# Attention into a feed-forward layer on one core: PSUM tiles handed out by the kernel, single-bank tiles for the block-form layer, one load cut into three, and a new order for every engine

## The chip, the cores and the metric

The kernel runs on one core of one Trainium2 chip. A core has a matrix engine (TensorE, PE in the profile), a vector engine (VectorE, DVE), an activation engine (ScalarE, ACT), GpSimd (POOL), which in this kernel issues the loads, and SyncE (SP), which issues transposing DMAs, copies and stores. Matmuls write to PSUM, a small memory of 128 partitions with eight banks of 512 fp32 values each; ACT and DVE read PSUM and write to SBUF. The metric is device time in microseconds (us). The kernel before takes 366.14 us, the median of three runs (365.94 to 366.96).

## The reference

```python
scores = (1/sqrt(64)) * q @ k.T             # q, k, v: 8 batches x 12 heads x 448 x 64, fp32
attn   = maximum(scores, 0)**2 / 448        # relu squared, no softmax
x      = (attn @ v).transpose(0, 2, 1, 3).reshape(3584, 768)
h      = x @ w_in                           # w_in: 768 x 2048
out    = gelu_exact(h) @ w_out              # w_out: 2048 x 768
```

Nothing is routed: every token goes through the same two layers. The kernel computes in bf16 with fp32 sums.

## The kernel before, in words

**Attention.** A batch has 12 heads in three groups of four (g = 0, 1, 2); below, (b, g) is group g of batch b. The loads of k, q and v (`add_k` L553, `add_q` L464, `add_v` L571) are cast to bf16 by the DMAs that POOL issues. q and k have to be turned so that the 64 head elements lie on the partitions. For batches 0 and 1 PE turns them and ACT or DVE copies the result out of PSUM (L520, L518). For batches 2 to 7 SP issues transposing DMAs (`turn`, L667), and the two halves of the turned q are swapped into a second copy (`swapped`): either by two DMAs of SP (L688, L689) or by two copies on DVE (L518). One attention step, "QK", is four matmuls of 448 columns (L744) into one two-bank PSUM tile; then relu with its scale on ACT (L756) or DVE (L758), then the square as a product on DVE (L765). Seven steps make a group of heads, whose 28 matmuls with v ("AV", L805) fill another two-bank tile; two copies (ACT L520 or DVE L518) bring it to x. Batch 0 is worked on in two halves of its queries, h0 and h1; its first q halves are loaded group by group, its second q halves by one load of 336 KB, `add_q(0, 0, G, HC, NC)`. In its own cost for a load (`add_q`) the kernel adds 390e3 bytes, one us at the rate that it assumes, to a load of this form.

**First layer.** Batches 0 to 3 are computed plainly: "F1", six matmuls of 448 columns for each of 16 blocks of 128 outputs (L857), then gelu on ACT (L867). Batches 4 to 7 use a block form of two by two blocks with seven products instead of eight (`add_blocks`, `add_block`, L1009). A block pair (b, m4) has two halves y = 0 and 1, and each half has three sums a, b, c that take in the products one after another; after each product DVE or ACT reads the sum (L1046, L520) before the next product is added to it. The gelu is L1055. The inputs are sums of blocks of x (`xs`) and of w_in (`ws`, L927), made on DVE.

**Second layer.** 14 row groups of 256 tokens. The first is done plainly (L1295), the others in the same seven-product form (`add_group`): eight matmuls for each product (L1191), copies and additions on ACT and DVE (L520, L1225), and stores issued by SP (L1145). Single-bank tiles come from the pool `f_pp` (two).

**PSUM.** The pool `w_pp` (L430) has three tiles of two banks, for QK, AV and the block form. `f_pp` (L431) has two tiles of one bank. In the block form, the two halves y of a sum share a tile of `w_pp`, one bank each; the tile comes free when both halves have been read (`joint`).

**The order.** The kernel is written as a list of operations (`sch.add`), and a string `ORDER` names every one of them in sequence: a letter for the engine (P, A, D, G for POOL, S) and the operation's number. `Scheduler.place` replays it, so each engine works through its operations in the string's order; within it an engine waits at the first one whose inputs are not ready. The string was made from the scheduler's own costs. With it PE alternates QK steps, AV and matmuls of the layers of earlier batches, so that relu and squares of one step run beside the layers' matmuls. POOL's loads wait in its queue, too: at most eight DMAs of POOL are under way at a time.

The lines of the code that set this:

```python
    w_pp = pool("w_pp", 3, PS)
    f_pp = pool("f_pp", 2, PS)
...
    add_q(0, 0, G, HC, NC)
    add_win(0)
    add_win(1)
```

Of the kernel before, what the change touches and what calls it, by code (L numbers as in the profile page):

```python
# [19 lines left out]
NA = 14  # L20
HP = H // 2
# [65 lines left out]
G0 G1 G3 G4 G1470 G7 A10 D13 A16 G121 P11 G2 P17 D12 D18 G117 P14 P42 D15 P39 G6 A43 P21 A40 P33  # L87
D22 P36 D44 P19 A37 P23 D20 G118 A34 D24 P25 G122 P54 D41 A26 G5 A55 P66 P57 Z1056 D67 A58 P63
P27 P29 A64 P69 D30 P48 D59 P31 A70 D28 D38 P78 A49 P51 D35 P133 G8 A52 D50 P45 D68 A79 P81 D53
A134 D46 P75 D47 G9 D65 A32 P131 A82 D56 P111 D132 A76 P108 D112 P129 G125 A109 D71 P102 P84 D103  # L90
G126 A85 P72 D80 P60 A73 D130 G120 A74 P93 D77 A61 P135 D104 A62 P96 D110 P105 A97 P141 D106 G147
A94 G124 D98 P165 A142 P90 P168 D107 A166 P143 D113 D86 A91 D83 P114 G119 A169 D92 P87 D115 A144
D95 A116 P171 D88 P137 A172 D89 P99 D138 A136 P159 P156 G128 D100 P145 D160 A157 D101 P162 A146
D173 P174 P186 G148 D175 P251 A187 D167 P243 A252 D170 A163 D158 P183 D188 A244 P189 P195 G150
P259 D184 A196 G154 A190 D176 P253 G151 D164 A260 G153 D161 P139 D191 P180 A140 P198 P177 D181
A199 D185 A254 P219 P216 G123 A178 P245 A220 G127 D179 S229 D182 P247 A246 A217 S228 P210 A248
P204 D218 P207 P263 A208 D205 P261 D211 A264 D197 S232 P192 A262 P213 D200 P222 A214 P255 D209
S231 A223 D193 P257 A256 D215 S235 P267 D206 A258 D194 S234 D221 P249 A268 D224 D212 P201 A250
P225 D230 G270 A202 A203 G238 P276 P279 A226 G149 D277 P265 A227 G239 A280 D233 P294 A266 P288
P291 A295 G152 P356 A289 P348 G272 G269 G271 P303 P285 A357 A292 A349 P350 A304 A286 P354 A351  # L100
D287 P312 P300 A355 P318 S399 P362 D281 D313 D296 P364 A363 D319 P370 D278 A301 A365 P358 A371
P315 P306 A359 P282 P352 D307 P360 A353 G241 P376 A361 P368 A377 A283 P366 A369 D284 D302 D236
# [82 lines left out]
class Scheduler:  # L185
# [170 lines left out]
    def place(self, fixed):  # L356
# [21 lines left out]
        while rest or any(fixed.values()):  # L378
# [16 lines left out]
            else:  # L395
                rest.remove(op)


@with_exitstack
def kernel(  # L400
    ctx: ExitStack,
# [388 lines left out]
    def add_av(blk, bias):  # L790
# [42 lines left out]
        if b in (B - 3, B - 1):  # L833
            old = [o for (bb, *_), o in AV.items() if bb == b - 1]
# [725 lines left out]
```

## Time and profile before

| what | value |
|---|---|
| runs | 366.14 us median of 3 (365.94 to 366.96) |
| span of the profiled execution | 365.2 us; its own time is some 0.9 us more, if it is taken for a median run (366.14 - 365.2) |
| PE busy | 356.2 us, 98% of the span, 3598 matmuls |
| DVE busy | 297.5 us, 81% |
| ACT busy | 208.2 us, 57% |
| POOL busy | 64.2 us, 18% |
| granted TensorE clock | 1.000 |

The times of the page are microseconds from the start of the span. "x28" is a number of instructions. "idle before it <- releaser" is the time for which the engine stood still ahead of an instruction, and what it had been waiting for. PEld is the loading of weights, which runs beside the matmuls. A DMA's row gives the issue on its queue; "landing" is when its data had arrived.

### The profile page before, as it was taken

The page shows a single profiled execution, that of the slowest core. Times are in us where ns is not written, and L with a number is a line of the kernel's source. Part 1 is how long each engine was busy: PE and PEld are TensorE (multiplying, and loading weights), DVE is VectorE, ACT ScalarE, POOL GpSimd, SP SyncE. Part 2 cuts the span into 40 slices and gives each one's busy share as a digit, 9 for nine tenths or more (in the row PEclk, how much of TensorE's full clock was granted, in tenths as well). Part 3 has the DMA queues.
Part 4 walks back from the last instruction along what each step waited for, and adds up shares of the span by engine and source line. Part 5 has one row for each costly group of instructions (what it writes and reads, how often), then busy time and mean ns, then how long its engine had stood idle before and what let it go on. Part 6 is the DMA issues. An engine that isn't in the chain of part 4 may idle for free.

```text
span 365.2 us, 8578 instructions
## 1 busy us (share of the span) xinstructions
PE 356.2 (98%) x3598; PEld 225.4 (62%) x3598; DVE 297.5 (81%) x510; ACT 208.2 (57%) x337; POOL 64.2 (18%) x101
## 2 busy tenths in 40 slices
PE   8799999999999999999999999999999999999996
PEld 4575644455454445555445555799787689788664
DVE  3899784399999988999899999999867847665764
ACT  5998868555767686766766677437027024425310
POOL 8575224160124125014000000000000000000000
PEclk9999999999999999999999999999999999999999
DMA  9999999999999999999792301002021200140223
GB/s 168 199 200 207 198 154 138 191 203 181 186 221 198 197 172 209 219 157 154 132 168 70 95 20 43 3 2 86 3 85 46 88 0 2 45 129 2 85 70 106
DMA packets 73126, 44.12 MB, mean 121 GB/s; under 512 B 38144, under 2 KB 69760, under 8 KB 73088
## 3 DMA queue, kind: packets, MB, share of 16 engines
q0 software_dynamic: 32912, 22.47, 42.7%
q1 hardware_dynamic: 39280, 20.26, 29.0%
q10 hardware_dynamic: 896, 0.85, 0.7%
q8 instruction: 28, 0.46, 0.5%
q14 instruction: 10, 0.08, 0.1%
HBM read 45.61 MB, written 11.01 MB: 155 GB/s over the span
## 4 chain that ended last, share of the span: by engine, by line
PE 78%; DVE 10%; DMA 7%; POOL 2%; issue 2%; ACT 1%; POOLq 0%; DVEq 0%
PE pso L1191 33%; PE pb L1009 18%; PE psh L857 14%; PE ps L744 7%; PE pav L805 6%; DMA win_sb<-in_moe_w_in_dram 5%; DVE a_sq L765 4%; DMA nq<-in_q_dram 2%; DVE t_sb L1120 1%; DVE a_sq L758 1%; DVE s_sb L1170 1%; DVE qT L518 1%; POOL nk L553 1%; ACT a_sq L756 0%; POOL win_sb L481 0%
## 5 line engine op out<-in xcount | busy, mean ns | idle before, releaser
L756 ACT ACTIVATE a_sq<-ps 128x896 bf16<-128x896 f32 (+1 forms) x125 | 110.3, 927 | 33.5 <-PE ps L744 33.4
L765 DVE TENSOR_TENSOR a_sq<-a_sq 128x896 bf16<-128x896 bf16 (+1 forms) x169 | 96.9, 614 | 11.8 <-ACT a_sq L756 11.3
L857 PE MATMUL psh<-xT,win_sb 128*128 128x448 bf16 (+1 forms) x420 | 77.6, 337 | 0.9 <-DMA win_sb<-in_moe_w_in_dram 0.9
L857 PEld LDWEIGHTS <-win_sb 128*128 128x128 bf16 x420 | 38.9, 98 | 37.3 <-issue 9.4
L1046 DVE TENSOR_TENSOR part<-pb,part 128x448 f32<-128x448 f32 x80 | 47.3, 619 | 15.9 <-PE pb L1009 14.2
L1191 PEld LDWEIGHTS <-s_sb 128*128 128x128 bf16 x424 | 40.5, 98 | 26.8 <-issue 2.4
L758 DVE TENSOR_SCALAR a_sq<-ps 128x896 bf16<-128x896 f32 (+1 forms) x44 | 47.1, 1074 | 9.2 <-PE ps L744 9.1
L744 PE MATMUL ps<-qT,kT 64*64 64x448 bf16 (+1 forms) x756 | 47.7, 336 | 1.6 <-ACT qT L520 0.5
L867 ACT ACTIVATE h_sb<-psh 128x448 bf16<-128x448 f32 x64 | 35.0, 552 | 20.8 <-PE psh L857 20.4
L1191 PEld LDWEIGHTS <-h_sb 128*128 128x128 bf16 x312 | 29.4, 98 | 21.6 <-issue 4.6
L1009 PEld LDWEIGHTS <-win_sb 128*128 128x128 bf16 x384 | 36.8, 98 | 2.7 <-issue 0.4
L1191 PE MATMUL pso<-wout_sb,h_sb 128*128 128x384 bf16 x208 | 38.1, 326 | 0.0
L1191 PE MATMUL pso<-t_sb,s_sb 128*128 128x384 bf16 x208 | 38.1, 326 | 0.0
L1191 PE MATMUL pso<-wout_sb,s_sb 128*128 128x384 bf16 (+1 forms) x208 | 37.6, 324 | 0.0
L805 PE MATMUL pav<-a_sq,v_sb 64*64 64x448 bf16 (+1 forms) x756 | 36.7, 329 | 0.6 <-DVE a_sq L765 0.2
L1055 ACT ACTIVATE h_sb<-part 128x448 bf16<-128x448 f32 x48 | 25.4, 575 | 14.6 <-DVE part L1046 14.6
L1225 DVE TENSOR_TENSOR osb<-pso,p_sb 128x384 f32<-128x384 f32 x39 | 21.5, 552 | 14.7 <-PE pso L1191 11.0
L744 PEld LDWEIGHTS <-kT 64*64 64x64 bf16 x756 | 18.8, 105 | 22.3 <-issue 16.3
L805 PEld LDWEIGHTS <-v_sb 64*64 64x64 bf16 x756 | 21.4, 107 | 11.9 <-issue 2.5
L464 POOL DMA_DIRECT2D nq<-in_q_dram x24 | 17.8, 744 | 59.9 <-DMA qT<-nq 55.2
L1009 PEld LDWEIGHTS <-ws 128*128 128x128 bf16 x288 | 27.6, 98 | 1.0
L1055 ACT ACTIVATE h_sb<-pb 128x448 bf16<-128x448 f32 x16 | 8.2, 541 | 29.3 <-PE pb L1009 29.2
(62 smaller groups left out, 327.1 us busy)
## 6 DMA issues: line engine op xcount, KB each, us to landing
nk<-in_k_dram POOLq DMA_DIRECT2D x23, 224.0 KB, 8.1
nq<-in_q_dram POOLq DMA_DIRECT2D x21, 224.0 KB, 7.0
v_sb<-in_v_dram POOLq DMA_DIRECT2D x5, 672.0 KB, 11.6
out_dram<-osb SPq DMA_DIRECT2D x7, 336.0 KB, 2.9
v_sb<-in_v_dram POOLq DMA_DIRECT2D x9, 224.0 KB, 9.9
out_dram<-osb SPq DMA_DIRECT2D x7, 288.0 KB, 3.3
out_dram<-osb SPq DMA_DIRECT2D x8, 240.0 KB, 3.0
win_sb<-in_moe_w_in_dram POOLq DMA_DIRECT2D x8, 192.0 KB, 9.6
```

Source lines behind the costliest of these rows:

```text
L744: nc.tensor.matmul(ps[64 * j : 64 * j + 64, e, x * w : x * w + w], kT[r, g, i * 128 + 64 * j : i * 128 + 64 * j + 64], moving, start=True, ...
L756: A.activation(ar, ps, AF.Relu, scale=c_att)
L758: V.tensor_scalar(ar, ps, c_att, 0.0, op0=mybir.AluOpType.mult, op1=mybir.AluOpType.max,)
L765: V.tensor_mul(box["a2"][:, :, :used], ar, ar)
L805: nc.tensor.matmul(pav[0][o2 : o2 + 64, e, :w], vt[b][r, 2 * g + e, bass.ts(i, D)], box["a2"][r, y, o : o + w], start=(i == 0), stop=(i == ...
L857: nc.tensor.matmul(ph[:, x * n : x * n + n], win_sb[:, kd, bass.ts(m + x, 128)], xT[b][:, kd, c], start=(kd == 0), stop=(kd == KD - 1),)
L867: A.activation(h_ring()[:, m : m + nm, o + c.start : o + c.stop], box[0][:, :S].rearrange("p (x n) -> p x n", x=nm), AF.Gelu,)
L1009: nc.tensor.matmul(bank[name][:, y, z * HS : z * HS + HS], w[:, k, bass.ts(mm, 128)], right()[:, k], start=first and k == 0 and z == 0, st ...
L1046: V.tensor_add(get(to), ps(name), get(other))
L1055: A.activation(h_ring()[:, m : m + 2, o + half[c].start : o + half[c].stop], src().rearrange("p (x n) -> p x n", x=2), AF.Gelu,)
L1191: nc.tensor.matmul(box[bank][:, n0:n1], left()[:, kf], right()[:, kf, n0:n1], start=bool(need) and kf == 0, stop=kf == K2 - 1, skip_group_ ...
L1225: V.tensor_add(out()[:, n0:n1], box[bank][:, n0:n1], other()[:, n0:n1])
```

## The change

1. `w_pp` goes. A class `Banks` allocates three two-bank tiles by name and hands them out itself: `take` gives the slot that has been free longest, `give` returns it when its last reader has been written down. QK's relu returns a QK tile, the second x copy an AV tile.
2. When the first product of the block form is reached, `Banks` closes that pool and opens one of six single-bank tiles ("u") in its place. Each half y of a block then has its own tiles for a, b and c, taken by the first product and returned by the last reader, without the `joint` release. All first products of blocks depend on every x copy of batch 7 (`ATT`). The short product "e" of the last group takes a single-bank tile as well.
3. Batch 0's second q halves are loaded by three loads of 112 KB, group by group. There are two operations more, and the numbers after them shift by two.
4. `ORDER` is new throughout. The matmuls are the same (485 operations on PE; PE changes between attention, layers and turns 122 times, 121 before). Read operation by operation, these differ:
   - POOL: `make_ident` comes first, ahead of the loads. Then q(0,1), k(0,1), k(0,2), the second half of group 0, q(0,2), the second halves of groups 2 and 1, k(1,1), v(0,0), v(0,1), q(1,0), k(1,0), v(0,2), the first two parts of w_in, k(1,2), q(1,1), parts 2 and 3 of w_in, q(1,2), v(1,0), q(2,0), part 4, q(2,1), k(2,0). Before, parts 2 and 3 stood behind q(1,2) and k(2,0); k(2,0) stood ahead of part 3.
   - The swaps of q: 14 of 18 are issued by SP (5 before) and 4 by DVE (13 before: groups 0 to 2 of batch 2 and group 0 of batch 3 stay there).
   - DVE has six more of the second layer's copies out of PSUM and two more relus (46 for 44), ACT six and two fewer.
   - PE: batch 2's first QK step comes ahead of AV(1,2) rather than behind it; AV(7,2) directly follows AV(7,1), and QK(7,2,3) is the last step ahead of these two. The first products "a" of several blocks come together right behind the attention, and the products of groups 5 and 6 come earlier.

```diff
+class Banks:
+    def __init__(self, tc, n, shape, space):
+        self.tc, self.space, self.stack = tc, space, None
+        self.open(n, shape)
+
+    def open(self, n, shape):
+        if self.stack:
+            self.stack.close()
+        self.stack = ExitStack()
+        self.shape, self.n = shape, n
+        name = f"w{n}_pp"
+        self.pool = self.stack.enter_context(
+            self.tc.tile_pool(name=name, bufs=1, space=self.space)
+        )
+        self.free, self.left, self.slot = list(range(n)), {}, {}
+
+    def take(self, name, uses=1):
+        x = self.free.pop(0)
+        t = self.pool.tile(self.shape, F32, tag=f"w{self.n}_{x}", name=name)
+        self.left[id(t)], self.slot[id(t)] = uses, (x, t)
+        return t
+
+    def give(self, t):
+        self.left[id(t)] -= 1
+        if not self.left[id(t)]:
+            self.free.append(self.slot[id(t)][0])
...
-    w_pp = pool("w_pp", 3, PS)
     f_pp = pool("f_pp", 2, PS)
+    banks = Banks(tc, NW, [128, 2, NB], PS)
...
-    sch = Scheduler({"w": 3, "a": NA, "f": 2, "osb": 3, "s1": 1, "s2": 1, "s3": 1, "s4": 1,
+    sch = Scheduler({"w": NW, "u": 2 * NW, "a": NA, "f": 2, "osb": 3, "s1": 1, "s2": 1, "s3": 1, "s4": 1,
...
-                ps = box["ps"] = w_pp.tile([128, 2, NB], F32, tag="w", name="ps")
+                ps = box["ps"] = banks.take("ps")
...
+                banks.give(box["ps"])
...
-            pav.append(w_pp.tile([128, 2, NB], F32, tag="w", name="pav"))
+            pav.append(banks.take("pav", 2))
...
-    def add_block(b, m4, y, ms, bank, x, t, TS, xs, half):
-
-        tmp = {}
+    def add_block(b, m4, y, ms, x, t, TS, xs, half):
+
+        tmp, ps = {}, {}
+        ATT = [o for (bb, *_), v in X.items() if bb == B - 1 for o in v]
...
-                if first and name not in bank:
-                    bank[name] = w_pp.tile([128, 2, NB], F32, tag="w", name="pb")
+                if first:
+                    if banks.n == NW:
+                        banks.open(2 * NW, [128, NB])
+                    ps[name] = banks.take("pb")
...
-                (("PE", d, d + 0.24),), fn, deps + bank.get(("first", name), []), mode="F",
-                need=("w",) if first and y == 0 else (),
+                (("PE", d, d + 0.24),), fn, deps + (ATT if first else []), mode="F",
+                need=("u",) if first else (),
...
-    add_q(0, 0, G, HC, NC)
+    for g in range(G):
+        add_q(0, g, g + 1, HC, NC)
...
 ORDER = """
-G0 G1 G3 G4 G1470 G7 A10 D13 A16 G121 P11 G2 P17 D12 D18 G117 P14 P42 D15 P39 G6 A43 P21 A40 P33
+G1472 A12 P13 A14 G1 D15 P16 D17 P23 G0 D24 P38 A18 P19 P35 G3 A20 G7 G4 D39 P21 D22 P41 G9 A36 P25
...
```

More of the change, by code (lines that the diff above doesn't have):

```diff
@@ L20 @@
 NA = 14
+NW = 3
 HP = H // 2
@@ L1364 @@
     A.activation(warm, warm, AF.Gelu)
[L1366 removed]
+    spin = banks.take("spin")
     for _ in range(SPIN):
```

215 lines of the change are left out of this document (106 added, 109 removed).

## The prediction

> **What bounds the kernel now.** I read the page's head first, then the span cut into stretches, then the chain of waits and PE's own waits.
>
> ```profile
> span 365.2 us, 8578 instructions
> PE 356.2 (98%) x3598; PEld 225.4 (62%) x3598; DVE 297.5 (81%) x510; ACT 208.2 (57%) x337; POOL 64.2 (18%) x101
> ```
>
> PE is busy for 98% of the span. The change leaves PE's matmuls alone, so only the 2% in which PE stands still can move, and what PE loses on starting late. The stretches tell where that is (columns: stretch, its length, then busy us and instructions of each engine, clock, DMA share, GB/s):
>
> ```profile
> 5.40:22.80 17.40, 14.34 (x397) 10.39 (x397) 15.46 (x31) 15.30 (x24) 12.23 (x19) 1.00 1.42 194
> 22.80:36.20 13.40, 12.53 (x211) 8.79 (x208) 12.94 (x25) 12.00 (x18) 8.12 (x13) 1.00 1.27 204
> 36.20:80.00 43.80, 43.80 (x410) 22.71 (x409) 28.80 (x44) 30.36 (x50) 15.04 (x22) 1.00 1.31 176
> 80.00:180.00 100.00, 99.64 (x971) 50.81 (x972) 93.56 (x156) 70.14 (x106) 23.68 (x40) 1.00 1.19 184
> 180.00:233.60 53.60, 53.60 (x536) 29.51 (x528) 51.49 (x87) 35.47 (x53) 0.85 (x1) 1.00 0.41 78
> 233.60:365.20 131.60, 128.15 (x1079) 101.76 (x1078) 94.66 (x170) 42.79 (x88) 0.00 (x0) 1.00 0.17 52
> ```
>
> Up to 36 us PE idles for 3.1 + 0.9 us, and there ACT and DVE are busy for 15 of 17 us: they empty PSUM as fast as PE fills it, or slower. From 36 us on PE hardly stops; the 3.45 us missing in the last row are the tail, stores after the last matmul, which stays. DVE is at 94 to 96% from 80 to 234 us, so a DVE result can come late there. The chain of waits shows what stood behind the start (start, length, what):
>
> ```profile
> 4.54 7.03 DMA nq<-in_q_dram
> 11.86 9.04 DMA win_sb<-in_moe_w_in_dram
> ...
> 25.35 10.47 DMA win_sb<-in_moe_w_in_dram
> 35.96 2.24 PE psh L857 x11
> ```
>
> The 336 KB load of q halves ends at 11.57, lets the first part of w_in be issued, and so on until PE's first layer waits for part 3 at 35.96. PE's own waits put a price on it (total, times, longest):
>
> ```profile
> PE psh L857 <- DMA win_sb<-in_moe_w_in_dram: 0.9, 2, 0.5
> PE tp L640 <- DMA nq<-in_q_dram: 0.8, 1, 0.8
> PE pav L805 <- DVE a_sq L765: 0.2, 1, 0.2
> ```
>
> No row of PE's waits names PSUM tiles of the block form, and PE's 233.6 to 365.2 stretch lacks nothing but the tail.
>
> **The change, part by part.** Durations of single operations, by shape (mean ns ahead of the last bar):
>
> ```profile
> L756 ACT ACTIVATE a_sq<-ps 128x896 bf16<-128x896 f32 x124 | 109.9, 930 | 32.3 <-PE ps L744 32.2
> L765 DVE TENSOR_TENSOR a_sq<-a_sq 128x896 bf16<-128x896 bf16 x167 | 96.3, 617 | 11.8 <-ACT a_sq L756 11.3
> L758 DVE TENSOR_SCALAR a_sq<-ps 128x896 bf16<-128x896 f32 x43 | 46.5, 1085 | 9.2 <-PE ps L744 9.1
> L518 DVE COPY qT<-qT 64x896 bf16<-64x896 bf16 x26 | 11.4, 439 | 0.7
> L1225 DVE TENSOR_TENSOR osb<-pso,p_sb 128x384 f32<-128x384 f32 x39 | 21.5, 552 | 14.7 <-PE pso L1191 11.0 <-ACT h_sb L1055 1.4 <-issue 1.4
> ```
>
> *Tiles handed out, single banks.* They take no instruction away and add none. Tiles come free sooner, and PE waited for none of them after 36 us: 0. That the new pool opens only when the last x copies are done costs 0 as long as second-layer products lie between; one stands there (8 matmuls, about 1.3 us) against two copies on ACT of 0.5 us each: 0 to +0.1, I take 0.
>
> *Three loads for one.* How long an issue takes to land (last number, median us), and the SP copies and turns for the parts below:
>
> ```profile
> nq<-in_q_dram POOLq DMA_DIRECT2D x1, 336.0 KB, 7.0
> nq<-in_q_dram POOLq DMA_DIRECT2D x2, 112.0 KB, 5.0
> qT<-qT SPq DMA_DIRECT2D x10, 112.0 KB, 5.5
> qT<-nq SPq DMA_TRANSPOSE x18, 6.1
> kT<-nk SPq DMA_TRANSPOSE x18, 6.8
> ```
>
> A 112 KB load lands 2 us sooner after its issue. POOL issues two DMAs more, at 0.7 us each, in a queue that later waits for landings anyway. I count the pieces as 1 us of the queue saved; between 0 and 2 us.
>
> The Trainium skill, "DMA: Bandwidth & Descriptors", section "Anatomy of one DMA", puts some 2.0 us of fixed cost on every DMA, and its rules say to coalesce small transfers. If those 2 us were paid one behind the other, two more DMAs would cost 4 us here, an estimate from that page; if they overlap, nothing. The rows (5.0 us for the small load, 7.0 for the large) fit the overlap better, but cannot exclude a part of it.
>
> *POOL's new order at the start.* Parts 2 and 3 of w_in move ahead of two 224 KB loads, so the two waits of PE for them, 0.9 us, go: −0.9. But what ACT and DVE have to do before the first F1 step is unchanged: summed in the order of the string, ACT's work up to the last x copy that F1 needs is 15.3 us in both, of the 17.4 us of the first row. PE comes to F1 with less behind it, and AV(0,0) and F1 wait for evictions instead. Following PE's, ACT's and DVE's queues with the durations above, the sum of these waits comes out about 0.5 us above that of the old order. It is the least certain term: −0.5 (the halves land earlier and DVE is ahead) to +1.5 (ACT alone decides). I take +0.5. Start together: −0.4.
>
> *Batch 2's first QK step ahead of AV(1,2).* It needs the turn of k(2,0), whose load now stands six places later.
>
> ```profile
> 42.53 1.32 SPq L667 DMA_TRANSPOSE qT<-nq  x1
> 43.90 2.46 SPq L667 DMA_TRANSPOSE kT<-nk  x1
> ...
> 52.11 0.73 POOL L464 DMA_DIRECT2D nq<-in_q_dram  x1 [10.45 <-DMA qT<-nq]
> 54.33 0.55 PE L744 MATMUL ps<-qT,kT 64*64 64x448 bf16 x8
> ```
>
> (The first two are rows of SP, then one of POOL and one of PE.) The turn issued at 42.53 had landed by 52.11: some 9 us while loads are under way, against the median of 6 to 7. After the change the loads up to k(2,0) are those up to q(2,0) now and one more, q(2,1): 224 KB at the 204 GB/s of the second stretch, 1.1 us. So k(2,0) lands where q(2,0) does now or 1.1 us later, 42.5 to 43.6, and its turn 6.8 to 9 us behind that, at 49.3 to 52.6. PE asks for it at about 52.0: 2.3 us of its work, AV(1,2) with 1.32 among it, move behind the first step, which starts at 54.33 now. Cost 0 to 0.6 us, and up to 1.5 if the turn is held up longer; I take +0.15, nearer to the median row.
>
> *AV(7,2) right behind AV(7,1).* The last QK step ahead of them is QK(7,2,3), and AV(7,2) needs it with its second matmul. One AV lies between:
>
> ```profile
> 214.85 1.32 PE pav L805 x28
> 226.19 1.49 PE L805 MATMUL pav<-a_sq,v_sb 64*64 64x448 bf16 x28
> ```
>
> From the end of the step: about 0.2 to ACT, relu 0.93, 0.1, square 0.62: 1.85 − 1.32 = +0.54. Before, AV(7,2) stood behind other work and had no wait.
>
> *Other close places.* Found the same way: AV(1,2) and the F1 step behind it (both x copies on ACT, only two QK steps between) 0.2, AV(4,1) and AV(6,2) 0.1 each: +0.4, between 0 and 1.0. One change of kind more on PE: +0.1.
>
> *Swaps from DVE to SP, copies and relus to DVE.* Nine swaps of 2 × 0.44 leave DVE (−7.9 us); six copies of 0.55 (+3.3) and two relus of 1.09 (+2.2) come: DVE has 2.4 us less. It pays only where PE waits for DVE. There are two such places:
>
> ```profile
> 94.78 0.54 PE L805 MATMUL pav<-a_sq,v_sb 64*64 64x448 bf16 x5
> 95.55 1.32 PE L805 MATMUL pav<-a_sq,v_sb 64*64 64x448 bf16 x23 [0.23 <-DVE a_sq L765]
> 96.53 0.54 PE L744 MATMUL ps<-qT,kT 64*64 64x448 bf16 x4
> ...
> 122.97 0.38 PE L744 MATMUL ps<-qT,kT 64*64 64x448 bf16 x4
> 123.49 1.52 PE L805 MATMUL pav<-a_sq,v_sb 64*64 64x448 bf16 x28
> ```
>
> The first AV takes 96.53 − 94.78 = 1.75 instead of 1.32, the second starts 0.52 behind four QK matmuls that need 0.2: 0.43 + 0.32 = 0.75. Both orders there are gone: −0.75. DVE stays above 90%, so I let a third come back in places that I cannot see: +0.25. On SP a swap lands in 5.5 us rather than 0.9. I looked at each of the 14: first use lies at least 8 us behind the turn's landing, so 0; without that cover up to 4 us.
>
> **The sum.** −0.4 + 0.15 + 0.54 + 0.4 + 0.1 − 0.75 + 0.25 = +0.29. Against the profiled execution: a span of 365.5 and, with the 0.9 us around it, 366.4; against the median of the runs, 366.14 + 0.29 = 366.4. That is +0.08%, no change: 0.3%, 1.1 us, is about what a measurement of this kernel can tell.
>
> **The rivals.**
>
> *Slower: a turn or swap comes late.* Place: QK of batch 2 (k(2,0)'s turn), or batch 3 to 7, where SP now carries 18 more copies. For it: the turn at 42.53 took some 9 us, and the DMA column of the stretches stands at 1.19 or more until 180 us. Against it: the swaps' cover of 8 us against 5.5. It decides once k(2,0)'s turn needs 9.5 us, or a swap 8. Price 1.5 to 3 us: 366.4 + 1.6 = 368.0.
>
> *Slower: small loads pay their start in line.* For it: nothing but the gap between 112 KB and 336 KB in the rows, if the larger load's 2 us were its own bytes only. Then three of them end 0.5 to 1 us later than the one, and everything that follows in the queue: PE's 0.9 us for w_in stay. Price: +0.9, 367.3. (This is the case of the fixed cost on the Trainium skill's page, "DMA: Bandwidth & Descriptors", section "Rules for kernel authors".)
>
> *Faster: the start gains what the chain says.* The chain runs through the queue of loads from 4.54 to 35.96. If the evictions follow the earlier q halves instead of ACT's own sum, the +0.5 becomes −0.75 and the close places shrink. Price: −0.9 − 0.75 for the start and −0.75 + 0.25 + 0.54 + 0.1 for the rest, 0.1 for the close places: −1.4, 364.7. Against it: ACT's 15.30 of 17.40 us.
>
> *The single banks do nothing.* It is contained in the forecast; I give no gain to them.
>
> **How the numbers follow.** The sum as it stands has 0.48, with its own range 365.4 to 367.2; its edges pass 0.3% a little, so 0.45 of it is no change, 0.02 slower and 0.01 faster. A late turn or swap: 0.22, slower. Small loads in line: 0.06, half above 367.24 and half below. Faster by the start: 0.19. A wait in the new order that I have not seen, over 1.1 us: 0.05, slower. Faster: 0.01 + 0.19 = 0.20. The same: 0.45 + 0.03 = 0.48. Slower: 0.02 + 0.22 + 0.03 + 0.05 = 0.32. The range leaves out the faster half of the faster case (0.09) and the worst of the late turns and unseen waits (0.1): 364.9 to 368.4.
>
> **What would show it.** Right: PE's waits name w_in no more; AV(7,2) shows about 0.5 us of idle behind DVE's square at about 222 us; the 180 to 234 us stretch has PE idle that it does not have now; the block form stays without idle time; the last matmul ends within a us of where it does now. Wrong: a wait of a QK step for a DMA near 52 us or later (late turn or swap); PE idle before 23 us well under 3.1 us (the faster case) or above 4; the chain running through SP's queue.

## The result, and the profile after

The changed kernel takes 367.97 us, the median of 8 runs (367.10 to 370.87), against 366.25 us for the kernel before (8 runs, 365.94 to 366.96). By the medians it is slower by 1.7 us, where the prediction had no change (366.4 us). The ratio is 1.0063, with a 95% interval of 1.0037 to 1.0089 (2.3 us; two of the eight executions took 370.7 and 370.9). The time lies in the predicted range, the sign doesn't. Ratios here and below leave out executions more than 1.5% above the fastest of their kernel (two of a_earlyv, one each of b_tail2 and h_new); medians and ranges keep them.

The head of the page of the kernel after, and its stretches (columns as before: stretch, its length, busy us and instructions of PE, PEld, DVE, ACT and POOL, clock, DMA share, GB/s):

```profile
span 365.3 us, 8602 instructions
PE 356.4 (98%) x3598; PEld 226.4 (62%) x3598; DVE 294.9 (81%) x500; ACT 203.2 (56%) x329; POOL 63.9 (18%) x103
```

```profile
5.40:22.80 17.40, 14.44 (x378) 10.19 (x379) 16.11 (x31) 15.26 (x24) 13.71 (x21) 1.00 1.40 195
22.80:36.20 13.40, 13.22 (x233) 9.27 (x234) 11.54 (x20) 11.89 (x20) 8.24 (x12) 1.00 1.29 203
36.20:80.00 43.80, 43.80 (x422) 22.24 (x417) 30.95 (x49) 33.47 (x54) 13.48 (x20) 1.00 1.30 192
80.00:180.00 100.00, 100.00 (x983) 51.98 (x982) 90.53 (x144) 65.50 (x97) 24.08 (x41) 1.00 1.15 180
180.00:233.60 53.60, 53.42 (x531) 30.00 (x530) 50.89 (x84) 34.85 (x53) 0.00 (x0) 1.00 0.65 119
233.60:365.20 131.60, 127.48 (x1054) 101.30 (x1052) 94.22 (x172) 40.17 (x82) 0.00 (x0) 1.00 0.17 49
```

Taken alone, the two profiles hide the loss: their spans are 365.2 and 365.3 us. The reason is in the times. In both, the execution's own time is 1.8 us more than its span (366.96 - 365.2 and 367.10 - 365.3), and 366.96 is the slowest of the eight runs of before while 367.10 is the fastest of after. So three more profiles of the old order are read beside that of before: b_banks, the kernel before with the new hand-out of tiles (experiment 2; 365.94 us, the fastest of its eleven), b_split, with the three loads (experiment 3; 366.11 us, the median of its eleven), and b_tail2, with two tiny loads more (experiment 4; 366.90 us, next to its median). The first two stretches of b_banks and its fourth:

```profile
5.40:22.80 17.40, 14.29 (x398) 10.38 (x398) 15.44 (x31) 15.37 (x25) 12.25 (x19) 1.00 1.43 196
22.80:36.20 13.40, 13.38 (x216) 9.26 (x213) 13.30 (x25) 12.36 (x18) 8.69 (x13) 1.00 1.27 204
...
80.00:180.00 100.00, 99.61 (x979) 50.80 (x978) 92.85 (x156) 69.66 (x105) 23.73 (x39) 1.00 1.23 186
```

From 22.8 to 36.2 us PE idles for 0.02 us here, for 0.10 in b_split and for 0.39 in b_tail2, not for the 0.87 us of the profile of before. The waits for w_in in this stretch are 0.9 us in before, 0.3 in b_tail2, and none is listed in the other two: most of the price that the prediction put on them belonged to one execution. From 80 to 180 us the old order loses 0.1 to 0.4 us (0.36, 0.39, 0.17 and 0.08), and the kernel after nothing.

PE's waits in the kernel after (total, times, longest):

```profile
PE ps L775 <- ACT a_sq L787: 1.2, 3, 0.5
...
PE psh L893 <- ACT xT L551: 0.5, 1, 0.5
PE tp L671 <- ACT qT L551: 0.4, 1, 0.4
```

w_in is gone from the list, as predicted, and evictions take more: QK's waits for ACT's relu are 1.2 us (0.4, 0.8, 0.7 and 0.9 in the four profiles of the old order), and the first F1 waits 0.5 us for ACT's x copy (none in the four).

**The end.** Both kernels end alike, with the same last store behind DVE's last addition. First the row of the kernel before, then that of the kernel after:

```profile
361.79 0.29 DVE L1225 TENSOR_TENSOR osb<-pse,osb 128x128 f32<-128x128 f32 x1
```

```profile
361.12 0.29 DVE L1256 TENSOR_TENSOR osb<-pse,osb 128x128 f32<-128x128 f32 x1
```

From DVE's end to the end of the span it takes 365.2 - 362.08 = 3.12 us before and 365.3 - 361.41 = 3.89 us after: the tail has grown by 0.77 us, though not one store differs. What fills it is SP's closing sequence, in us before the end of the span (SP waits for the completion semaphores of its own and ACT's DMAs one after another, in a fixed sequence, some 0.06 us each):

```
                                        before              after
last DMA of SP and ACT has landed       -1.05               -1.84
SP's waits behind that landing          -1.03 to -0.91 (3)  -1.82 to -1.36 (8)
SP's DRAIN, next DRAIN                  -0.85, -0.78        -1.29, -0.89
```

These DMAs share eight completion semaphores in turn. Before, SP and ACT issue 111 of them, 13 x 8 + 7, so the last one uses the seventh semaphore and SP has already passed most of the row when it lands. The nine swaps that went from DVE to SP make 18 more: 129 = 16 x 8 + 1. The last one uses the first semaphore, and the whole row is waited for behind it. (The numbers of the table are read from the semaphore events of the two traces.)

**AV(7,2).** The two AVs at the end of the attention, in the kernel after:

```profile
225.57 1.67 PE L837 MATMUL pav<-a_sq,v_sb 64*64 64x448 bf16 x29
227.42 1.51 PE L837 MATMUL pav<-a_sq,v_sb 64*64 64x448 bf16 x27 [0.18 <-DVE a_sq L797]
```

The 56 matmuls take 227.42 + 1.51 - 225.57 = 3.36 us; without a wait they take 2.98 (a row of that stands with experiment 8).

**The start.** PE's second matmuls on q, the turn of the load q(0,1), in the kernel after and, below it, in another execution of the same kernel (a_again):

```profile
6.38 0.39 PE L671 MATMUL tp<-ident,nq 112*64 112x112 bf16 x8 [0.40 <-ACT qT L551]
```

```profile
7.38 0.39 PE L671 MATMUL tp<-ident,nq 112*64 112x112 bf16 x8 [1.12 <-DMA nq<-in_q_dram]
```

POOL issues this load first of all, at 1.46 us, and over the eleven profiles of the new start it lands between 5.84 and 7.80 us. In the kernel after itself it landed at 5.84, and PE waited for ACT's copy, not for it. The old order loads k(0,1) first, and comes to these matmuls at 7.2 us:

```profile
7.22 0.39 PE L672 MATMUL tp<-ident,nq 112*64 112x112 bf16 x8
```

(This row is of the kernel before with the new hand-out.)

### The profile page after: what moved, and what is told of

The parts are those of the page before. It is cut to its first block, busy times and chain, and to the rows that moved or that the text cites. A ratio compares the mean times of both kernels' runs of the same rounds, so it can differ in the third digit from the quotient of the medians.

```text
span 365.3 us, 8602 instructions
## 1 busy us (share of the span) xinstructions
PE 356.4 (98%) x3598; PEld 226.4 (62%) x3598; DVE 294.9 (81%) x500; ACT 203.2 (56%) x329; POOL 63.9 (18%) x103
## 4 chain that ended last, share of the span: by engine, by line
PE 94%; DVE 2%; ACT 1%; DMA 1%; issue 0%
PE pso L1222 33%; PE psh L893 21%; PE pb L1045 18%; PE ps L775 10%; PE pav L837 8%; PE pso L1328 3%; DVE a_sq L797 2%; DMA q<-in_q_dram 1%; ACT a_sq L787 1%; PE tp L671 1%; PE tp L643 0%; ACT kT L551 0%; DVE osb L1256 0%; DVE qT L549 0%; ACT nq L551 0%
## 5 line engine op out<-in xcount | busy, mean ns | idle before, releaser
L787 ACT ACTIVATE a_sq<-ps 128x896 bf16<-128x896 f32 (+1 forms) x123 | 108.1, 924 | 30.6 <-PE ps L775 30.5
L893 PE MATMUL psh<-xT,win_sb 128*128 128x448 bf16 (+1 forms) x420 | 78.6, 337 | 0.5 <-ACT xT L551 0.5
L789 DVE TENSOR_SCALAR a_sq<-ps 128x896 bf16<-128x896 f32 (+1 forms) x46 | 49.5, 1077 | 11.9 <-PE ps L775 11.7
L1076 DVE TENSOR_TENSOR part<-pb,part 128x448 f32<-128x448 f32 x80 | 46.5, 617 | 10.9 <-PE pb L1045 8.3
L775 PE MATMUL ps<-qT,kT 64*64 64x448 bf16 (+1 forms) x756 | 49.0, 337 | 1.4 <-ACT a_sq L787 1.2
L837 PEld LDWEIGHTS <-v_sb 64*64 64x64 bf16 x756 | 22.8, 107 | 11.5 <-issue 2.2
L495 POOL DMA_DIRECT2D nq<-in_q_dram x26 | 19.0, 736 | 47.5 <-DMA qT<-nq 42.6
L1045 PE MATMUL pb<-xs,win_sb 128*128 128x224 bf16 x192 | 23.3, 259 | 0.0
```

The costliest lines, as they stand in the source:

```text
L775: nc.tensor.matmul(ps[64 * j : 64 * j + 64, e, x * w : x * w + w], kT[r, g, i * 128 + 64 * j : i * 128 + 64 * j + 64], moving, start=True, ...
L787: A.activation(ar, ps, AF.Relu, scale=c_att)
L789: V.tensor_scalar(ar, ps, c_att, 0.0, op0=mybir.AluOpType.mult, op1=mybir.AluOpType.max,)
L837: nc.tensor.matmul(pav[0][o2 : o2 + 64, e, :w], vt[b][r, 2 * g + e, bass.ts(i, D)], box["a2"][r, y, o : o + w], start=(i == 0), stop=(i == ...
L893: nc.tensor.matmul(ph[:, x * n : x * n + n], win_sb[:, kd, bass.ts(m + x, 128)], xT[b][:, kd, c], start=(kd == 0), stop=(kd == KD - 1),)
L1045: nc.tensor.matmul(ps[name][:, z * HS : z * HS + HS], w[:, k, bass.ts(mm, 128)], right()[:, k], start=first and k == 0 and z == 0, stop=k ...
```

## The experiments

Ratios are to the kernel before in runs on the same chip, with their 95% interval. In `ORDER` a word is an engine and an operation.

**1. The kernel after once more (a_again).** No edit.

> The changed kernel once more, unchanged, for a second profiled execution and for more spans. The one profiled so far has a span of 365.3 us and a time of 367.10, the fastest of its eight runs (median 367.97, two at 370.7 and 370.9). If those runs are longer by a wait that comes and goes (theory A: a late turn or swap, or a lower granted clock in some executions), then runs between 367.0 and 371 appear again, and the spans differ while time less span stays at 1.8 us. If the cost lies outside the span (theory B), time less span is larger than for the kernel before.

Measured: 367.88 us (367.60 to 369.49, 6 runs), 1.0049 [1.0030, 1.0067]. The slowdown repeats, and time less span stays at 1.7 to 1.8 us, so the cost lies inside the span. The profiled execution took 369.49 us (span 367.7); beside the 1.12 us above, it shows loads of batch 4 arriving just late:

```profile
136.59 1.52 PE L837 MATMUL pav<-a_sq,v_sb 64*64 64x448 bf16 x28 [0.17 <-DMA v_sb<-in_v_dram]
138.30 0.57 PE L775 MATMUL ps<-qT,kT 64*64 64x448 bf16 x8 [0.20 <-DMA kT<-nk]
```

In seven profiles of the new order with these loads in place v(4) lands 0.05 to 3.9 us ahead of AV(4,0) (1.2 in the kernel after, 0.05 here), in the four of the old order 7.6 to 10.6 us. The turn of k(4,2) lands 0.05 to 4.9 us ahead of its QK step where the trace tells it, in the old order more than 10 us ahead. Four of the 14 runs of this kernel lie above 369.4 us; of the 91 of the kernel before in all sets of runs none does, and the highest took 369.34.

**2. The hand-out of tiles alone (b_banks).** The kernel before; three two-bank tiles handed out by `Banks`, the halves of the block form still sharing one.

```diff
-    w_pp = pool("w_pp", 3, PS)
     f_pp = pool("f_pp", 2, PS)
+    banks = Banks(tc, 3, [128, 2, NB], PS)
...
-                ps = box["ps"] = w_pp.tile([128, 2, NB], F32, tag="w", name="ps")
+                ps = box["ps"] = banks.take("ps")
...
-                    bank[name] = w_pp.tile([128, 2, NB], F32, tag="w", name="pb")
+                    bank[name] = banks.take("pb", 2)
```

> The kernel before with its three two-bank tiles handed out by the kernel (Banks), the block form still with shared two-bank tiles, the order as before. The prediction gives 0 to this: 366.25 within 0.3 us. If handing out costs or saves waits on the PSUM tiles, or changes what lies behind the last instruction, the difference shows: up to 1.5 us.

Measured: 366.36 us (365.94 to 368.07, 11 runs), 1.0002 [0.9990, 1.0014]. The hand-out costs and gains nothing. Single-bank tiles were not tried with the old order by themselves.

**3. The three loads alone (b_split), and taken out of the new order (a_oneload).** For the first, the kernel before with

```diff
-    add_q(0, 0, G, HC, NC)
+    for g in range(G):
+        add_q(0, g, g + 1, HC, NC)
...
-G0 G1 G3 G4 G1470 G7 A10 D13 A16 G121 P11 G2 P17 D12 D18 G117 P14 P42 D15 P39 G6 A43 P21 A40 P33
+G0 G1 G3 G4 G1472 G7 G8 G9 A12 D15 A18 G123 P13 G2 P19 D14 D20 G119 P16 P44 D17 P41 G6 A45 P23 A42
```

and for the second the kernel after with the reverse (one load at the place of G7).

> The kernel before with batch 0's second q halves in three loads, nothing else. If the small loads overlap, as the prediction's sum has it, PE waits less at the start: -0.3 to -1.0 us, 365.3 to 366.0. If their fixed part is paid in line: 0 to +0.9 us. If three more or fewer DMAs make no difference behind the start: within 0.3 us of 366.25.

> The changed kernel with the one load of 336 KB back in the place of the first of the three small ones. If the small loads save 1 us of the queue and PE's start follows it: +0.3 to +1.0 us against the changed kernel, 368.3 to 369.0. If the small loads are what makes it slower: 366.3 to 367.5.

Measured: b_split 366.11 us (365.35 to 366.58, 11 runs), 0.9991 [0.9982, 1.0001]; a_oneload 370.25 us (369.77 to 375.15, 6 runs), 1.0122 [1.0084, 1.0161]. In the old order the three loads land at 9.44, 10.06 and 10.72 us, the single one at 10.60 to 11.56; that is worth 0.3 us there by the ratio, and not told from nothing. The new order needs them: with one load PE stands still for it,

```profile
10.57 0.39 PE L671 MATMUL tp<-ident,nq 112*64 112x112 bf16 x8 [1.19 <-DMA nq<-in_q_dram]
```

and later for v(4) and v(5), 0.36 and 0.27 us.

The rival "small loads pay their start in line" falls: the pieces land 0.62 and 0.66 us apart, which is 112 KB at some 180 GB/s, near the 195 GB/s of the first stretch, and the last of them lands within the times of the whole. The Trainium skill, "DMA: Bandwidth & Descriptors", section "Rules for kernel authors", advises to coalesce many small transfers and counts those under 64 KB as mostly overhead; at 112 KB a piece, no run here shows a cost of cutting.

So neither the hand-out nor the loads: what is left is the order, and the single-bank tiles, which were not run apart. PE's stretch with the block form has no idle time in the kernel after (below), so what follows is about the order.

**4. The end of the new order with more DMAs (a_tail7), that of the old order too (b_tail2).** Behind a store of row group 6, some 90 to 100 us ahead of the end, seven (or two) loads of four bytes more on SP's queue: 136 and 113 DMAs.

```diff
-            return lambda e: store_rows(rows[x][0] // 128, osb(x), c, queues)
+            def fn(e):
+                store_rows(rows[x][0] // 128, osb(x), c, queues)
+                if g == 6 and x == 0:
+                    for n in range(7):
+                        nc.sync.dma_start(warm[8 * n : 8 * n + 1], q[0, 0, n : n + 1, :1])
+            return fn
```

> The changed kernel with seven loads of 4 bytes more on SP's queue, issued behind a store of group 6; nothing reads them. The program's DMAs of SP and ACT take eight completion semaphores in turn, and at the end SP waits for them one by one. In the changed kernel there are 129 such DMAs, so the last store has the first semaphore of the row and eight waits of some 0.06 us and a drain stand behind its landing (1.84 us from landing to the end, against 1.04 before, where the row's seventh is the last). With 136 the last store has the eighth. Theory A (the row's order makes the longer tail): the stretch from PE's last matmul to the end falls from 4.25 to about 3.4 to 3.6, the time to about 367.2. Theory B (the tail is longer for another reason, such as the stores' own time): no change, 367.9.

> The kernel before with two loads of 4 bytes more on SP's queue, behind a store of group 6, which nothing reads. Its 111 DMAs of SP and ACT become 113, so the last store has the first of the eight semaphores, as in the changed kernel. Theory A (the position of the last store's semaphore in SP's final row of waits costs 0.8 us, whatever the order): the stretch from PE's last matmul to the end grows from 3.46 to about 4.25, the time to 367.0. Theory B (it belongs to the new order's stores): no change, 366.3.

Measured: a_tail7 367.58 us (366.56 to 369.53, 11 runs), 1.0034 [1.0016, 1.0052]; b_tail2 366.86 us (366.14 to 373.06, 11 runs), 1.0020 [0.9997, 1.0043]. The span and DVE's last row of a_tail7, then of b_tail2:

```profile
span 365.3 us, 8609 instructions
361.90 0.29 DVE L1256 TENSOR_TENSOR osb<-pse,osb 128x128 f32<-128x128 f32 x1
```

```profile
span 365.1 us, 8580 instructions
361.41 0.29 DVE L1225 TENSOR_TENSOR osb<-pse,osb 128x128 f32<-128x128 f32 x1
```

365.3 - 362.19 = 3.11 us: seven DMAs more, and the tail is as short as before. 365.1 - 361.70 = 3.40 us, though the times of b_tail2 do not tell it from no change: two more than the old order's 111, 14 x 8 + 1, and the tail grows by 0.3 us, as eight waits behind a landing instead of three should (5 x 0.06). Over all nineteen profiles of this case, the time from DVE's end is 3.1 to 3.2 us with 111 or 136 DMAs and 3.4 to 4.0 us with 113 or 129. The other 0.4 us of the 0.77, at SP's two DRAINs, come only in kernels of the new order with 129 DMAs. An 8 KB fetch of instructions stands 0.13 to 0.27 us ahead of the end in those kernels, earlier, later or not at all in the ones without the gap; that SP crosses a boundary of its program there is a guess, not shown. By their times alone a_tail7 (1.0034) and a_again (1.0049) are not told apart; experiment 8 does that.

**5. AV(7,2) by itself (a_av72).** QK(7,2,3) moves ahead of the second-layer product in front of the two AVs.

```diff
-... P866 P1014 A1015 ...
+... P1014 P866 A1015 ...
```

> The changed kernel with QK(7,2,3) moved ahead of one eight-matmul product of group 6, so that 1.3 us more lie between it and AV(7,2). The prediction priced this wait at 0.54 us; the profile shows the step 0.64 late. Expected: -0.5 to -0.65 us, 367.3. If DVE or the PSUM tiles hold AV(7,2) instead, nothing changes.

Measured: 369.36 us (368.19 to 370.30, 6 runs), 1.0082 [1.0062, 1.0102]. A miss: the wait at AV(7,2) is gone (its 56 matmuls with AV(7,1) take 2.98 us), the time is longer. In the profiled execution q(0,1) landed at 7.80 us, the latest of all, and PE waited 1.04 us for it. Whether that holds for all six runs is not known. Experiment 8 makes the same move and is not slower for it, and from PE's 123rd operation on (experiment 9) PE ends 0.18 us sooner than in the kernel after, so nothing shows that the move costs. Why the runs were slower stays open.

**6. The swaps back on DVE (a_dveswap), and loads earlier (a_earlyv).** First, the nine swaps that went to SP return to DVE, some 4.5 us of PE's work ahead of their first use (the lines below have one of them); then v(4) and v(5) are loaded six and seven places earlier in POOL's queue (the lines have v(4), G418).

```diff
-... S404 S403 S405 A424 P425 ...
+... S404 S403 D405 A424 P425 ...
```

```diff
-... S551 G416 A540 ... D630 G418 P623 ...
+... S551 G418 G416 A540 ... D630 P623 ...
```

> The changed kernel with the nine swaps of q that it moved to SP done by DVE again (batch 3 groups 1 and 2, batch 4, batch 5 groups 0 and 2, batch 6 groups 0 and 1), about 4.5 us of PE work ahead of their first use. Theory A (a swap on SP waits for a turn's landing and holds up the next turn, and with it POOL's loads; besides, 18 DMAs less put the last store on the row's seventh semaphore again): k(4,2)'s turn is issued some 5 us sooner, the loads of v(4) and v(5) land at least 3 us ahead of AV(4,0) and AV(5,0), the tail falls by 0.8; together 366.6 to 367.2. Theory B (DVE, with 7.9 us more work, is now late for PE): 368 or more, with waits of PE for DVE between 95 and 170 us.

> The changed kernel with two loads earlier in POOL's queue: v(4) ahead of k(4,2), and v(5) ahead of the loads of batch 6. In two of three profiles of this order PE waits 0.2 to 0.6 us at AV(4,0) or AV(5,0) for these loads, which land 0.04 to 1.2 us ahead of use. Theory A (late loads make the typical run slower than the fast one): -0.2 to -0.6 us, 367.4, and fewer runs above 368. Theory B (the late loads only matter in rare runs): 367.9 unchanged; or the loads now delay k(4,2) and its turn, which would add waits at QK(4,2).

Measured: a_dveswap 371.50 us (371.02 to 371.98, 4 runs), 1.0140 [1.0119, 1.0161]; a_earlyv 371.52 us (367.63 to 377.37, 6 runs), 1.0108 [1.0067, 1.0150]. With 111 DMAs again a_dveswap has a short tail (3.5 us from the last matmul, as before), but DVE now comes late in QK and AV:

```profile
PE ps L775 <- DVE a_sq L789: 1.3, 3, 0.5
...
PE pav L837 <- DVE a_sq L797: 1.0, 3, 0.7
```

With the swaps at these places, their way to SP was needed in this order; its price is in the tail. Loading v(4) and v(5) sooner did not help either. The profiled execution of a_earlyv is the slowest of its six (377.37 us), and how far it stands for the others is not known. In it other transfers come late in place of v. At the third row below PE waits for a turn of k that landed 9 us after its issue. At the second it waits for DVE, which had waited 2.2 us for a store on SP's queue. At the first a turn of k had landed 14 us after its issue, half a us ahead of the row, and ACT came last.

```profile
126.81 0.51 PE L775 MATMUL ps<-qT,kT 64*64 64x448 bf16 x4 [1.45 <-ACT h_sb L903]
147.61 1.46 PE L1222 MATMUL pso<-t_sb,h_sb 128*128 128x384 bf16 x8 [1.79 <-DVE osb L1256]
153.27 1.25 PE L775 MATMUL ps<-qT,kT 64*64 64x448 bf16 x8 [2.56 <-DMA kT<-nk]
```

**7. PE's second operation later (a_start).** The turns of q(0,1) (P23) and of a part of k (P21), with their copies, move behind the third QK step.

```diff
-G1472 A12 P13 A14 G1 D15 P16 D17 P23 G0 D24 P38 A18 P19 P35 G3 A20 G7 G4 D39 P21 D22 P41 G9 A36 P25
+G1472 A12 P13 A14 G1 D15 P16 D17 G0 P38 A18 P19 P35 G3 A20 G7 G4 D39 P41 P23 D24 P21 D22 G9 A36 P25
```

> The changed kernel with PE's turns of q(0,1) and k(0,1) behind the third QK step of group 0 instead of ahead of the first and third. In seven profiles of the new order PE waits 0.5 to 1.4 us for the load of q(0,1) at about 6.4 us, its second operation; in three of the old order, where it asks at 7.2, 0. Theory A (this wait is what makes the typical start of the new order 0.5 to 1.5 us later than the old one's): the wait at the turn of q(0,1) falls below 0.3 us, PE's lag at 36 us from 5.6 to 7.1 to about 5.3 to 6.0, the time from 367.9 to 367.0 to 367.4. Theory B (ACT and DVE set the start, and the wait only takes time that PE would lose later): PE's lag at 36 us stays at 6.4 or more, the time at 367.9.

Measured: 368.80 us (368.52 to 369.61, 5 runs), 1.0077 [1.0065, 1.0089]. The wait for the load is gone, and others stand there:

```profile
7.33 0.39 PE L775 MATMUL ps<-qT,kT 64*64 64x224 bf16 x8 [0.53 <-DVE kT L549]
...
8.58 0.39 PE L775 MATMUL ps<-qT,kT 64*64 64x224 bf16 x8 [0.26 <-ACT kT L551]
```

A wait moved is not a wait removed: neither theory gave this time. What the start follows can be read in the seven profiles that keep the new start (with h_new): PE turns the third load, k(0,2), 0.04 to 0.13 us behind its landing, and that lies anywhere from 8.33 us (the kernel after) to 9.99 us (a_av72). In a_start it landed at 9.72. (At the turn of q(0,1) itself PE waits for the load in four of the seven, 0.5 to 1.1 us, and for ACT's copy in three.) No run changes this load by itself.

**8. On top of it the tail, then AV(7,2) (a_start_tail, a_start_tail_av).** The edits of experiments 4 and 5.

> The changed kernel with both edits: the turns of group 1 later and seven DMAs of 4 bytes more, so that the last store has the eighth semaphore. If both theories A hold and add up: 367.9 - 0.7 - 0.8 = 366.4, the same as before. If only the tail counts: 367.1 to 367.5.

> These two edits and QK(7,2,3) one product earlier. In the profile of that edit alone the late AV(7,2) went from 0.64 to 0.27, but its runs were slower (369.4) than those of the changed kernel, which I cannot explain from its profile. If the slower runs came from its start (0 to 1.4 us of waiting for q(0,1)), which is out of the way here: 365.9, at or below the kernel before. If the move itself costs something: above a_start_tail by 1 us or more.

Measured: 367.82 us (367.39 to 368.68, 5 runs), 1.0049 [1.0037, 1.0062], and 367.37 us (367.18 to 368.93, 6 runs), 1.0041 [1.0026, 1.0056]. Against a_start, the tail is worth 1.0 us. AV(7,2) is worth 0.45 us more by the medians, with intervals that overlap; in the traces PE ends 0.18 us sooner, as in a_av72. Its two AVs run through:

```profile
226.80 2.98 PE L837 MATMUL pav<-a_sq,v_sb 64*64 64x448 bf16 x56
```

**9. Starts exchanged (h_new, h_old, h_old_tail_av, h_old2, h_old2_tail_av).** After PE's 123rd operation, at some 85 us, both orders have given PE the same operations. There the two are joined: h_new is the kernel before, with the three loads, in the new order up to that point and the old order from there; h_old is the kernel after in the old order up to that point. h_old2 leaves POOL's loads in the new order from the 33rd on; "tail_av" adds the edits of experiments 4 and 5. For h_new:

```diff
-G0 G1 G3 G4 G1472 G7 G8 G9 A12 D15 A18 G123 P13 ...
+G1472 A12 P13 A14 G1 D15 P16 D17 P23 G0 D24 P38 ...
```

> The mirror of it: the kernel before with the three small loads, every engine in the new order up to PE's 123rd operation and in the old order from there on; 111 DMAs of SP and ACT as before. Theory A: slower than the kernel before by 0.6 to 1.0 us, 1.0015 to 1.003, with the first load's wait and QK's waits for relu in the first 25 us as in the kernel after, and a tail of 3.5 us. Theory B: 0.999 to 1.001.

> The kernel after, with every engine following the order of the kernel before up to PE's 123rd operation (all of batch 0 to 2's attention and F1 up to some 70 us; at this point both orders have given PE the same 123 operations), and the new order from there on. Theory A (about 0.75 us of the loss arises before 36 us, where the second operation of PE waits for the first load and evictions come late): the time falls by 0.6 to 1.0 us against the kernel after, to a ratio of 1.002 to 1.0035 against the kernel before; the tail still reads about 4.25 us from the last matmul to the end, AV(7,2) is still 0.6 us late. Theory B (the start costs nothing, all of the loss is tail, AV(7,2) and the later loads): unchanged, 1.0045 to 1.0055.

> The old order's start as in the first kernel of this set, seven four-byte loads more on SP behind a store of the last but one group, and QK(7,2,3) ahead of the product in front of AV(7,2). If start, tail and AV(7,2) are the whole of the loss, this equals the kernel before: a ratio of 0.999 to 1.001. If something else in the order from 70 us on costs (the late v(4), v(5) loads, DVE), it stays at 1.002 or more.

> As h_old, but POOL takes its loads in the new order and at the new places from the 33rd on, so that batch 3's k is not loaded behind two parts of w_out that the old order put ahead of it (in h_old PE stood still for 3.0 us on that turn of k). Theory A (the start costs some 0.5 to 0.75 us, as the mirror kernel had it with 0.2%): 1.002 to 1.0035 against the kernel before, no wait of QK for a turn over 1 us. Theory B (the start costs nothing): 1.0045 to 1.0055. If a turn of k is late again, the seam and not the start decides, and the run says nothing on it.

> The same, with seven four-byte loads more on SP and QK(7,2,3) ahead of the product in front of AV(7,2). If start, tail and AV(7,2) are the whole of the loss: 0.999 to 1.001. If something else from 70 us on costs: 1.002 or more.

Measured: h_new 366.98 us (366.17 to 372.47, 12 runs), 1.0019 [1.0004, 1.0034]. The new start costs 0.5 us by the medians, 0.7 by the ratio. Its waits are those of the kernel after:

```profile
7.25 0.39 PE L638 MATMUL tp<-ident,nq 112*64 112x112 bf16 x8 [0.50 <-DMA nq<-in_q_dram]
...
12.98 0.39 PE L742 MATMUL ps<-qT,kT 64*64 64x224 bf16 x8 [0.46 <-ACT a_sq L754]
14.60 0.39 PE L742 MATMUL ps<-qT,kT 64*64 64x224 bf16 x8 [0.31 <-ACT a_sq L754]
...
60.63 0.38 PE L742 MATMUL ps<-qT,kT 64*64 64x448 bf16 x4 [2.53 <-DMA kT<-nk]
```

The profiled execution was the slowest of its runs: the last row, where a turn of k in batch 2 came 2.5 us late, is the place of the rival "a turn or swap comes late", met once.

The times of the other four tell nothing on the start: h_old 372.66 us, 1.0172 [1.0137, 1.0207]; h_old_tail_av 372.19, 1.0166 [1.0137, 1.0195]; h_old2 373.43, 1.0190 [1.0144, 1.0236]; h_old2_tail_av 372.73, 1.0150 [1.0115, 1.0185]. At the seam PE stands still once, for 3.0 to 3.7 us. In h_old and h_old_tail_av it waits for a turn of k; in the two others the row names no releaser. The row of h_old:

```profile
88.07 0.65 PE L775 MATMUL ps<-qT,kT 64*64 64x448 bf16 x8 [3.02 <-DMA kT<-nk]
```

They show two things beside. h_old issues 129 DMAs like the kernel after, and from DVE's last row to its end it takes 369.5 - 366.06 = 3.44 us, the 0.3 us of the semaphores without the 0.4 of the DRAINs:

```profile
span 369.5 us, 8593 instructions
365.77 0.29 DVE L1256 TENSOR_TENSOR osb<-pse,osb 128x128 f32<-128x128 f32 x1
```

And the stall can cost more than its length. The stretches of h_old around it:

```profile
84.00:88.00 4.00, 1.05 (x9) 0.34 (x7) 3.94 (x7) 0.01 (x1) 0.00 (x0) 1.00 1.26 172
88.00:90.00 2.00, 1.93 (x35) 1.86 (x38) 1.97 (x4) 1.43 (x3) 0.48 (x1) 0.83 0.68 134
90.00:92.00 2.00, 2.00 (x16) 0.79 (x9) 1.97 (x3) 1.60 (x2) 2.00 (x4) 0.50 0.65 111
92.00:94.00 2.00, 2.00 (x12) 1.09 (x11) 2.00 (x4) 0.00 (x0) 1.19 (x2) 0.82 1.33 212
94.00:96.00 2.00, 2.00 (x14) 1.20 (x13) 2.00 (x5) 0.48 (x1) 0.00 (x0) 1.00 1.26 204
```

The granted clock falls to a half from about 89.3 to 92.7 us: 2 x (0.17 + 0.50 + 0.18) = 1.7 us lost beyond the 3.0.

The traces price the start without the seam, too. Up to PE's 123rd operation both orders have issued the same 1066 matmuls. The next one begins, in b_banks and then in the kernel after, each the fastest execution of its kernel:

```profile
84.61 1.49 PE L838 MATMUL pav<-a_sq,v_sb 64*64 64x448 bf16 x28
```

```profile
85.12 0.57 PE L775 MATMUL ps<-qT,kT 64*64 64x448 bf16 x8
```

In the four profiles of the old order it begins at 84.6 to 85.6 us, in six of the new order (the kernel after, a_again, a_tail7, a_av72, a_dveswap, a_earlyv) at 85.1 to 86.7. The means are 85.2 and 86.1: the new start costs 0.9 us, give or take half a us for so few profiles. From there to the end of the last matmul the old order takes 275.8 to 276.2 us and the new one as much: 275.96 in the kernel after, 275.95 in a_tail7. Only a_again, with its late loads of batch 4, takes 276.71. So behind the start the waits gained and lost on PE come out even, and only the tail is added.

## Why the prediction was wrong

Two steps failed: the start, forecast at -0.4 us and measured at +0.5 to +0.9, and the tail, put at nothing and measured at +0.8. Point by point, by the prediction's own steps:

- *Tiles handed out, single banks: 0.* Right: 1.0002 for the hand-out, and the stretch from 233.6 us on has no idle time in the kernel after but the tail (131.60 - 127.48 = 4.12).
- *Three loads: 1 us of the queue.* Within its range and of no use in the old order (0.9991): the last piece landed at 10.72 us in b_split, the whole load at 10.60 to 11.56.
- *Start together: -0.4.* This step failed, by its sign: +0.5 to +0.7 by h_new's times, +0.9 by the traces at PE's 123rd operation. Its part "the waits for w_in go: -0.9" was priced from the one profile of before; three others of the old order idle for 0.02 to 0.39 us between 22.8 and 36.2 us, so there was little to gain. The part "evictions +0.5" fits in size (QK's waits for relu 1.2 us against 0.4 to 0.9, and 0.5 for the x copy, against waits for the turned q of the old order that are gone in part). What the sum did not hold at all is the landing of the first loads: `make_ident` and q(0,1) come first and PE asks for q(0,1) 0.8 us earlier than in the old order (6.4 for 7.2 us), while that load lands at 5.8 to 7.8 us and k(0,2), right behind which PE works, at 8.3 to 10.0. That these landings are the cause is read from the profiles and not tested by a run.
- *k(2,0)'s turn: +0.15.* About right for the usual execution, none in the kernel after; one execution of h_new lost 0.4 us there and 2.5 us at a turn behind it.
- *AV(7,2): +0.54.* Right in kind, too large: the two AVs take 3.36 - 2.98 = 0.38 us more, PE idles for 0.18, and moving the step ends PE 0.18 us sooner in two traces.
- *Other close places: +0.4.* Not found as such: from 36 to 180 us PE has no idle time in the kernel after. In some executions batch 4's loads come late instead (0.17 + 0.20 us of waits in a_again), which the prediction did not look at: its cover was measured for swaps, and v(4) and k(4,2)'s turn had lost much of theirs.
- *DVE's two waits -0.75, a third +0.25.* The waits are gone and no third came: 100.00 busy of 100 us, against 99.61 to 99.92 in the four profiles of the old order. That is 0.1 to 0.4 us, at most about half the size: the stretch of before had 0.36 us of idle time (99.64 of 100), not 0.75, which a look at its row would have told.
- *"The 3.45 us missing in the last row are the tail, stores after the last matmul, which stays."* This step failed, too: a term that the prediction put at nothing. The tail grew by 0.77 us (0.78 in the rows of experiment 4, 1.0 by the times of experiment 8), and the cause was in the change's own list: the step on the swaps counted what SP's copies cost while they run, and not that 18 DMAs more shift the semaphore on which the last store completes.
- *"A span of 365.5 and, with the 0.9 us around it, 366.4."* Wrong: 1.8 us lie around the span, and the profiled execution was 0.7 us above the median. The two mistakes all but cancelled in the forecast, by luck, but the second is what made the gain at w_in look real.

The sum that the runs support: tail +0.8, start +0.5 to +0.9, the rest of PE's time 0 (the wait at AV(7,2) against DVE's waits that are gone), late loads of batch 4 in some executions: +1.3 to +1.7 and those, against +1.7 by the medians (with an interval of 1.4 to 3.3 by the ratio's 1.0037 to 1.0089, or 1.1 to 2.5 by a_again's). Within the scatter of a few profiles the account closes. No run shows it in one: the kernel with tail and AV(7,2) mended and the old start, which should have equalled the kernel before, could not be had without the stall at the seam. Of the rivals, "a turn or swap comes late" had the sign and about the time (368.0 for 367.97), but that is luck and not the cause of the median: late turns were met in single executions. No kernel tried is faster than the kernel before; b_split, 0.9991 [0.9982, 1.0001], is the same.

## What to carry to other kernels

Work that is moved between engines is to be followed to the very end of the kernel: an order with more DMAs on SP ended 0.8 us later with not one store changed. One profile is one execution: set its own time against the runs before pricing a wait in it, and price a gain from a profile that stands at the median. And an order that takes the slack out of loads loses time in single executions, where a stall of PE of some 3 us can cost 1.7 us more in clock.

## What the runs showed of the hardware

- SP closes the kernel by waiting for eight completion semaphores in a fixed sequence, 0.06 us each; which of them the last DMA uses is set by the count of SP's and ACT's DMAs modulo eight, and moves the end by 0.3 us (111 against 113 in the old order: 3.12 and 3.40 us). In the kernel after 0.4 us more lie at SP's two DRAINs; the cause is open.
- The first load that POOL issues in the new order, at 1.46 us, lands 4.4 to 6.3 us later, from one execution to the next (eleven profiles). The first load of the old order, of k(0,1), issued at 1.24 us, lands at 6.18 to 6.33 us in eight profiles; its second varies from 6.8 to 7.5 us.
- PE's clock falls to a half for 3.41 us around a stall of 3.0 us (h_old), and in the executions of h_new and a_earlyv shown around stalls of 2.5 and 2.6 us. It did not fall for stalls of 1.8 us and less (a_earlyv), and of two stalls of 3.29 us one brought the fall (h_old2) and one did not (h_old2_tail_av). The Trainium skill, "TensorE: Matmul & The Clock Gate", section "Part 1: The HAM clock gate", lets the clock fall after an idle window of about 3.4 us that runs freely; the length of the slow time agrees, but here stalls shorter than the window were enough.
